# Three PSUM banks for the first layer's products, and a bank shared by two tiles of the second

## The chip, the cores and the metric

One core of a Trainium2 chip runs the kernel. The metric is the device time of one execution in microseconds; the median of several runs is given.

## The reference

```python
def _attn_ref(x, filt_r, filt_i):          # x: 8 x 2496 x 256
    X = np.fft.rfft(x, axis=1)
    Y = X * (filt_r + 1j * filt_i)[None, :, :]
    return np.fft.irfft(Y, n=x.shape[1], axis=1).astype(np.float32)

def _moe_ref(x, w_gate, w_noise, noise, w1, w2):   # x: 19968 x 256, 8 experts, 1024 hidden
    noisy_logits = x @ w_gate + np.log1p(np.exp(x @ w_noise)) * noise
    top2 = np.argpartition(-noisy_logits, 2, axis=1)[:, :2]
    ...                                    # top2_w: softmax of the two logits
    for e in range(E):
        for k in range(2):
            mask = top2[:, k] == e
            h = np.maximum(x[mask] @ w1[e], 0.0)
            out[mask] += top2_w[mask, k, None] * (h @ w2[e])
```

A filter along the sequence (FFT, product, inverse FFT) gives 19968 rows of 256. Each row then goes through two of eight experts, each a layer of 256 x 1024, a relu, and a layer of 1024 x 256.

## The kernel before

The FFT is done as matrix products, batch by batch (eight batches), and its rows are written to a DRAM table `y`. Routing makes, for each expert, lists of rows. The expert part (`expert`) then works through these lists in blocks of 512 rows (`nt` = 4 tiles of 128), all of one expert. A list entry holds one such block, in a later stage two with the same weights (a pair, the second has `i` = 1), and at the end what is left over is done in units of 256 rows (`nt` = 2). For each block:

- `gather`: POOL fetches the rows of `y` with indirect DMAs, one a tile (line 954), into eight slots of `stage`. `front` loads the weights and `turn` transposes the rows on TensorE (PE, line 970, bank `xps`); ACT and DVE take the result to SBUF.
- Layer one: for each f of 0 to 7, 128 of the 1024 hidden units, six matmuls make a product of 128 x 512. All operands are split in a high and a low part, and a product is high x high, low x high and high x low (`_mm3`, lines 119 to 121), for two halves of the 256 inputs. ACT applies the relu and writes the high part `hh` (line 1051), DVE computes the low part `hl` (line 1052), and both read the product's PSUM bank. With every second f, ACT and DVE split a quarter of the second layer's weights (`wsplit`, lines 1014 and 1015), if the block is the first with these weights.
- `turn` or `front` of the next block.
- Layer two: for each tile t of 128 rows, 24 matmuls (3 for each f) add up in one PSUM tile of 128 x 256 (`yps`). ACT reads it, scaled by the gate, into one of six slots `yo` of `stage` (line 1073), and POOL adds it to the output with an indirect DMA (line 1074). "Reading" or "scatter" below mean these two.

PSUM has eight banks of 128 x 512 floats. The names (tags) hold them so: `hps` two, `yps` two, `xps` one, `fps` three. A tile of half a bank takes a whole one. After the early part the FFT and the routing use `fps` alone. In the units, odd f take `fps` too, under the name `hq`, so that the first layer there has up to five banks.

The order in which each engine does its instructions is fixed when the kernel is built. Tile, the library below, walks a simulated timeline (`schedule_with_timeline_sim=True`): whenever an engine is free in it, the instruction that comes first in the program among those that are ready there goes next. So instructions of layer two, of the next block or of the FFT stand in PE's queue between those of layer one where the simulated bank was not free. On the chip the queues run in that order, and an instruction waits for what it needs. The same library gives out the banks of a tag and puts in the waits.

FFT steps are handed out between the expert steps (`run`, at each `yield` of `expert`), by a pace that counts these steps.

Of the kernel before, what the change touches and what calls it, by code (L numbers as in the profile page):

```python
# [10 lines left out]
F32 = mybir.dt.float32  # L11
# [9 lines left out]
NB, S, D = 8, 2496, 256  # L21
# [96 lines left out]
def _mm3(nc, o, lh, ll, rh, rl, start=True, stop=True):  # L118
    nc.tensor.matmul(o, lh, rh, start=start, stop=False)  # L119
    nc.tensor.matmul(o, lh, rl, start=False, stop=False)  # L120
    nc.tensor.matmul(o, ll, rh, start=False, stop=stop)  # L121


def f32v(ap):
    return ap.bitcast(F32)
# [13 lines left out]
class Moe:  # L139
# [885 lines left out]
    def expert(self, parts, may, fill=None):  # L1025

        nc, P = self.nc, self.P
        self.parts, self.ahead = parts, []
        self.fetch(lambda: True)
        cur = None  # L1030
        while self.ahead:
            blk, i, xg = self.ahead.pop(0)
            lt, n, nt, s, tabi, ready = blk
            w = 128 * nt
            if cur is None:
                cur = self.front(blk, xg, fill)
            w1, xT, w2st = cur
            if i == 0:
                w2, adds = [], []
            ids, gate = lt[:, i], xT[2]  # L1040
            self.fetch(may)
            hh = []
            for f in range(8):
                p = (self.ps("hq") if nt < 4 and f % 2 else self.PS.tile([128, 512], F32, name="hps", bufs=2))[:, :w]
                for kc in range(2):
                    wh, wl = w1[f // 2]
                    o = (f % 2) * 128
                    _mm3(nc, p, wh[:, kc, o:o + 128], wl[:, kc, o:o + 128], *xT[kc], start=(kc == 0), stop=(kc == 1))
                h = P.tile([128, 512], R32, name="hh", bufs=8)[:, :w]
                l = P.tile([128, 512], R32, name="hl", bufs=8)[:, :w]  # L1050
                nc.scalar.activation(h, p, AF.Relu)  # L1051
                nc.vector.scalar_tensor_tensor(l, p, 0.0, f32v(h), op0=ALU.max, op1=ALU.subtract)  # L1052
                hh.append((h, l))
                if f % 2 and i == 0:
                    w2.append(self.wsplit(w2st[f // 2], "w2", f // 2))
                yield
            late = not self.ahead
            if late:
                self.fetch(lambda: True)
            if self.ahead:  # L1060
                b2, i2, x2 = self.ahead[0]
                cur = (w1, self.turn(x2, nt), None) if i2 else self.front(b2, x2, fill if late else None)
            self.fetch(may)
            yield
            for t in range(nt):
                p = self.PS.tile([128, D], F32, name="yps", bufs=2)
                for f in range(8):
                    h, l = hh[f]
                    wh, wl = w2[f // 2]
                    _mm3(nc, p, h[:, t * 128:(t + 1) * 128], l[:, t * 128:(t + 1) * 128], wh[:, f % 2], wl[:, f % 2],  # L1070
                         start=(f == 0), stop=(f == 7))
                o = self.slot("yo")
                nc.scalar.activation(o, p, AF.Copy, scale=gate[:, t])  # L1073
                a = nc.gpsimd.indirect_dma_start(  # L1074
                    out=self.io["out"][:BLK + ready * ROWS], out_offset=bass.IndirectOffsetOnAxis(ap=ids[:, t:t + 1], axis=0),
                    in_=o, in_offset=None, compute_op=ALU.add)
                for q in adds:
                    self.tc.declare_no_dep(a.ins, q.ins, reason="distinct rows of one expert")
                adds.append(a)
                self.lasta = a  # L1080
                yield
# [108 lines left out]
```

## Time and profile before

| | |
|---|---|
| runs shown | 2447.89, 2452.72, 2455.28 us; median 2452.72 |
| the profiled execution | 2450.5 us, its span 2448.7 us |
| granted TensorE clock, mean | 0.988 |
| instructions in the profile | 43571 |
| busy: PE, DVE, ACT, POOL | 2336.5, 1471.5, 1183.8, 949.0 us |
| HBM | 219.38 MB read, 103.08 MB written |

The profile shows one execution. PE is TensorE's matmuls and PEld its weight loads, DVE is VectorE, ACT ScalarE, POOL GpSimd. A row of a group has the line, the engine, the operation, what it writes and reads (`out<-in`), the shapes, the count, and then busy time, the mean of one in ns, and the idle time of the engine ahead of it with what ended it. The names of buffers have no numbers, so the two `yps` banks look alike. A row of the waits has the waiting engine and instruction, what it waited for, and us in total, how often, and the longest. Matmuls overlap: one of 256 columns shows 0.28 us, but the next starts 0.12 us after it; one of 512 columns shows 0.39 us, and the next starts 0.23 us after it.

### The profile page before, as it was taken

How to read it: one execution, taken by the hardware profiler on the slowest of the kernel's cores; microseconds unless marked ns; L12 is line 12 of the kernel's file. 1: busy time of each engine (PE TensorE's matmuls, PEld its weight loads, DVE VectorE, ACT ScalarE, POOL GpSimd, SP SyncE). 2: the span in 40 equal slices, each digit the busy share in tenths (PEclk: the TensorE clock that was granted, in tenths of full speed). 3: DMA queues.
4: the chain of work that ended last, by engine and by line, in shares of the span. 5: the costliest groups of instructions: out<-in, count | busy, mean ns of one | idle time of the engine just before them, and what ended most of it. 6: DMA issues, size and time to landing. Idle time of an engine off the chain costs nothing. (4 is left out here: it accounts for less than half of the span.)

```text
span 2448.7 us, 43571 instructions
## 1 busy us (share of the span) xinstructions
PE 2336.5 (95%) x15299; PEld 2047.7 (84%) x15299; DVE 1471.5 (60%) x3243; ACT 1183.8 (48%) x2364; POOL 949.0 (39%) x837
## 2 busy tenths in 40 slices
PE   8878989989999999999999999999999999999998
PEld 6547877878888888887888888888888888999998
DVE  5868787787687567668668333334333434446775
ACT  5454645645554554553544344333333444446775
POOL 3123332323333333333333434453445344545553
PEclk9989999999999999999999999999999999999999
DMA  8265746746646555544544344443444344558774
GB/s 268 85 194 151 197 122 167 199 110 187 151 112 152 132 141 129 131 129 101 118 121 93 79 87 90 89 85 85 94 85 87 86 93 101 140 140 231 223 220 96
DMA packets 276350, 324.60 MB, mean 133 GB/s; under 512 B 36870, under 2 KB 189086, under 8 KB 276126
## 3 DMA queue, kind: packets, MB, share of 16 engines
q1 hardware_dynamic: 214046, 236.30, 31.9%
q0 software_dynamic: 62080, 85.47, 20.9%
q8 instruction: 122, 2.00, 0.3%
q14 instruction: 102, 0.84, 0.1%
HBM read 219.38 MB, written 103.08 MB: 132 GB/s over the span
## 5 line engine op out<-in xcount | busy, mean ns | idle before, releaser
L119 PE MATMUL yps<-w2h,hh 128*128 128x256 f32 x2560 | 717.0, 289 | 24.8 <-ACT hh L1051 24.7
L1052 DVE SCALAR_TENSOR_TENSOR hl<-hps,hh 128x512 fp32r<-128x512 f32 (+1 forms) x640 | 417.3, 656 | 534.8 <-ACT hh L1051 467.5
L120 PE MATMUL yps<-w2l,hh 128*128 128x256 f32 x2560 | 703.0, 283 | 0.0
L1074 POOL DMA_INDIRECT out<-stage,ids x320 | 527.0, 1647 | 380.9 <-ACT stage L1073 312.1
L954 POOL DMA_INDIRECT stage<-y,ids x320 | 330.6, 1033 | 872.0 <-PE xps L970 492.0
L121 PE MATMUL yps<-w2h,hl 128*128 128x256 f32 x2560 | 645.1, 283 | 1.3 <-DVE hl L1052 1.2
L1051 ACT ACTIVATE hh<-hps 128x512 fp32r<-128x512 f32 (+1 forms) x640 | 363.8, 574 | 343.4 <-PE hps L121 328.4
L119 PEld LDWEIGHTS yps<-w2h,hh 128*128 128x128 f32 x2560 | 489.7, 191 | 47.9 <-ACT hh L1051 32.4
L119 PE MATMUL hps<-mxh,w1h 128*128 128x512 f32 (+1 forms) x1280 | 489.2, 391 | 26.1 <-DVE hl L1052 21.2
L121 PEld LDWEIGHTS yps<-w2h,hl 128*128 128x128 f32 x2560 | 478.6, 191 | 36.2 <-DVE hl L1052 2.1
L120 PE MATMUL hps<-mxl,w1h 128*128 128x512 f32 (+1 forms) x1280 | 497.3, 389 | 0.1
L120 PEld LDWEIGHTS yps<-w2l,hh 128*128 128x128 f32 x2560 | 490.1, 192 | 8.0
L121 PE MATMUL hps<-mxh,w1l 128*128 128x512 f32 (+1 forms) x1280 | 492.9, 385 | 0.0
L1073 ACT ACTIVATE stage<-yps,gt 128x256 f32<-128x256 f32 x320 | 142.7, 474 | 400.8 <-issue 185.1
L119 PEld LDWEIGHTS hps<-mxh,w1h 128*128 128x128 f32 x1280 | 243.4, 191 | 70.0 <-DVE hl L1052 32.2
L121 PEld LDWEIGHTS hps<-mxh,w1l 128*128 128x128 f32 x1280 | 242.7, 190 | 43.6
L120 PEld LDWEIGHTS hps<-mxl,w1h 128*128 128x128 f32 x1280 | 242.9, 190 | 26.3 <-DVE mxl L975 0.5
L1015 DVE TENSOR_TENSOR w2l<-stage,w2h 128x512 fp32r<-128x512 f32 x216 | 141.1, 687 | 66.5 <-ACT w2h L1014 63.0
L1014 ACT CAST w1h<-stage 128x512 fp32r<-128x512 f32 x180 | 111.7, 621 | 116.2 <-PE hps L120 85.2
L1015 DVE TENSOR_TENSOR w1l<-stage,w1h 128x512 fp32r<-128x512 f32 x180 | 123.3, 686 | 66.2 <-ACT w1h L1014 65.4
L975 DVE TENSOR_TENSOR mxl<-xps,mxh 128x512 fp32r<-128x512 f32 (+1 forms) x178 | 112.8, 634 | 71.0 <-ACT mxh L974 70.1
L974 ACT CAST mxh<-xps 128x512 fp32r<-128x512 f32 (+1 forms) x178 | 96.9, 544 | 119.5 <-PE xps L970 62.7
(212 smaller groups left out, 2794.3 us busy)
## 6 DMA issues: line engine op xcount, KB each, us to landing
stage<-w SPq DMA_DIRECT2D x396, 256.0 KB
x<-x SPq DMA_DIRECT2D x88, 256.0 KB
wb<-w SPq DMA_DIRECT2D x18, 1024.0 KB
out<-z SPq DMA_DIRECT2D x24, 702.0 KB
fd<-c SPq DMA_DIRECT2D x66, 240.0 KB
fx<-fd SPq DMA_DIRECT2D x120, 128.0 KB
y<-yt SPq DMA_DIRECT2D x40, 248.6 KB
y<-yt SPq DMA_DIRECT2D x40, 234.0 KB
```

What stands on the lines that cost most here:

```text
L119: nc.tensor.matmul(o, lh, rh, start=start, stop=False)
L120: nc.tensor.matmul(o, lh, rl, start=False, stop=False)
L121: nc.tensor.matmul(o, ll, rh, start=False, stop=stop)
L954: self.pin(lambda: self.nc.gpsimd.indirect_dma_start(out=x, out_offset=None, in_=self.y[:BLK + ready * ROWS], in_offset=bass.IndirectOffse ...
L974: nc.scalar.copy(h, q[:, :w])
L975: nc.vector.tensor_sub(l, q[:, :w], f32v(h))
L1014: nc.scalar.copy(h, sv)
L1015: nc.vector.tensor_sub(l, sv, f32v(h))
L1051: nc.scalar.activation(h, p, AF.Relu)
L1052: nc.vector.scalar_tensor_tensor(l, p, 0.0, f32v(h), op0=ALU.max, op1=ALU.subtract)
L1073: nc.scalar.activation(o, p, AF.Copy, scale=gate[:, t])
L1074: a = nc.gpsimd.indirect_dma_start(out=self.io["out"][:BLK + ready * ROWS], out_offset=bass.IndirectOffsetOnAxis(ap=ids[:, t:t + 1], axis= ...
```

## The change

In layer one, f = 2 and f = 5 take a bank of the tag `yps`, in blocks and in units alike; the other six take `hps`, and `hq` is gone. In layer two, tiles 0 and 1 of a block share one PSUM tile of 128 x 2 x 256, a whole bank, and tiles 2 and 3 the next one; ACT reads each half when its 24 matmuls are done. The number of banks of each tag stays.

```diff
             for f in range(8):
-                p = (self.ps("hq") if nt < 4 and f % 2 else self.PS.tile([128, 512], F32, name="hps", bufs=2))[:, :w]
+
+                p = self.PS.tile([128, 512], F32, name="hps", tag="hps" if f % 3 < 2 else "yps", bufs=2)[:, :w]
                 for kc in range(2):
...
             for t in range(nt):
-                p = self.PS.tile([128, D], F32, name="yps", bufs=2)
+
+                if t % 2 == 0:
+                    bank = self.PS.tile([128, 2, D], F32, name="yps", bufs=2)
+                p = bank[:, t % 2]
                 for f in range(8):
```

## The prediction

> **What bounds the kernel now.** I read the busy shares first, then the stretches by stage, then who waited for whom on TensorE, and last the order of single instructions around one such wait.
>
> ```profile
> PE 2336.5 (95%) x15299; PEld 2047.7 (84%) x15299; DVE 1471.5 (60%) x3243; ACT 1183.8 (48%) x2364; POOL 949.0 (39%) x837
> 0.00:200.00 200.00, 159.66 (x913) 107.92 (x914) 141.24 (x432) 103.25 (x205) 47.59 (x50) 0.95 0.60 179
> 200.00:700.00 500.00, 470.82 (x2975) 402.95 (x2974) 374.43 (x817) 268.35 (x525) 174.28 (x148) 0.98 0.62 161
> 700.00:1400.00 700.00, 684.62 (x4429) 596.06 (x4428) 475.11 (x1174) 325.79 (x639) 251.23 (x215) 0.99 0.50 119
> 1400.00:2050.00 650.00, 633.60 (x4048) 568.93 (x4048) 243.28 (x372) 252.63 (x479) 287.03 (x255) 1.00 0.41 88
> 2050.00:2190.00 140.00, 140.00 (x909) 127.09 (x908) 69.32 (x108) 68.99 (x132) 66.42 (x58) 1.00 0.57 134
> 2190.00:2449.00 259.00, 247.85 (x2033) 244.76 (x2032) 168.11 (x343) 164.82 (x387) 122.40 (x112) 0.99 0.67 190
> ```
>
> The columns of a stretch are its length, then busy time of PE, PEld, DVE, ACT and POOL, the granted clock, the DMA share and GB/s. PE is the bound from 200 us on. The experts run beside the FFT until 1400, alone in pairs of blocks until 2050, in single blocks until 2190 and in units of 256 rows to the end. From 2050 on PE has no idle time (the last stretch ends in the write-out). So the change can only win what PE idles between 200 and 2050, and only the part that waits for a bank or for the engines that empty one. Here are PE's own waits, for the three stretches in order, two rows each, and after them the same two waits on the weight loads over the whole run (us in total, times, longest).
>
> ```profile
> PE hps L119 <- DVE hl L1052: 14.0, 12, 3.1
> PE yps L119 <- ACT hh L1051: 3.9, 7, 1.3
> ...
> PE yps L119 <- ACT hh L1051: 6.0, 6, 1.7
> PE hps L119 <- DVE hl L1052: 4.7, 6, 1.8
> ...
> PE yps L119 <- ACT hh L1051: 14.8, 14, 1.2
> PE hps L119 <- DVE hl L1052: 1.6, 5, 0.4
> ...
> PEld yps L119 <- ACT hh L1051: 32.4, 31, 2.0
> PEld hps L119 <- DVE hl L1052: 32.2, 49, 3.3
> ```
>
> A first-layer product that waits for DVE's `hl` wants its bank back. A second-layer product that waits for ACT's `hh` has been put in early, as filler between first-layer products. Together PE lost 17.9, 10.7 and 16.4 us, 45.0 in all, and 64.6 counted on the weight loads, which stop first. These two sums are the ends of what can be won.
>
> How such a filler comes to wait is seen in one pair of blocks (start, duration, and in brackets idle time before):
>
> ```profile
> 1595.60 0.28 PE L121 MATMUL yps<-w2h,hl 128*128 128x256 f32 x1
> 1595.97 0.47 ACT L1073 ACTIVATE stage<-yps,gt 128x256 f32<-128x256 f32 x1 [3.31 <-issue]
> 1598.48 0.28 PE L121 MATMUL yps<-w2h,hl 128*128 128x256 f32 x1
> 1598.69 1.59 POOL L1074 DMA_INDIRECT out<-stage,ids  x1 [0.30 <-issue]
> 1599.53 0.60 PE L970 MATMUL xps<-ident,stage 128*128 128x128 f32 x4
> 1600.25 0.47 ACT L1073 ACTIVATE stage<-yps,gt 128x256 f32<-128x256 f32 x1 [3.81 <-PE hps L121]
> 1600.62 0.59 ACT L1051 ACTIVATE hh<-hps 128x512 fp32r<-128x512 f32 x1
> 1601.27 0.38 PE L119 MATMUL yps<-w2h,hh 128*128 128x256 f32 x1 [1.14 <-ACT hh L1051]
> ```
>
> At 1595.60 the third tile of a block ends, and ACT reads it 0.09 us after the matmul's end. The fourth ends at 1598.76, but ACT reads it only at 1600.25, as POOL's scatter of 1598.69 comes to its end. The relu behind it on ACT's queue is late by that much, both `hps` banks are full, and the next thing written into PE's order is a second-layer product that needs this relu. PE stands 1.14 us.
>
> **The change part by part.** *The third bank for layer one.* No matmul, evacuation or DMA is added or taken away: f = 2 and 5 of a block move from `hps` (or from `fps`, in units) to `yps`. A full bank costs this:
>
> ```profile
> 1632.39 0.39 PE L119 MATMUL hps<-mxh,w1h 128*128 128x512 f32 x1
> 1633.09 0.39 PE L119 MATMUL hps<-mxh,w1h 128*128 128x512 f32 x1
> 1633.55 0.39 PE L121 MATMUL hps<-mxh,w1l 128*128 128x512 f32 x1
> 1633.97 0.60 ACT L1051 ACTIVATE hh<-hps 128x512 fp32r<-128x512 f32 x1 [1.50 <-PE hps L121]
> 1634.61 0.69 DVE L1052 SCALAR_TENSOR_TENSOR hl<-hps,hh 128x512 fp32r<-128x512 f32 x1 [1.41 <-ACT hh L1051]
> ```
>
> Three matmuls are issued in 0.70 us, so a product of six takes 1.40. The last one leaves PE's issue at 1633.55 + 0.23 = 1633.78, DVE is done at 1635.30: 1.52 us to empty a bank. With two banks one product (1.40) stands between a bank's use and its reuse, which is 0.12 too little, and so filler has to stand there: both first tiles of layer two in turn. With three banks two products stand there, 2.80 us, and 1.28 us of lateness costs nothing. The first layer then needs no filler, and no filler has to wait for the first relu. A lateness like the one above (1600.25 against about 1598.85, 1.40 us) would cost 0.1 instead of 1.14. Behind this stands the load of ACT and DVE in a denser first layer: 0.60 + half a weight cast on ACT, 0.69 + half a split on DVE for each 1.40 us:
>
> ```profile
> L1014 ACT CAST w2h<-stage 128x512 fp32r<-128x512 f32 x52 | 29.7, 628 | 0.0
> L1015 DVE TENSOR_TENSOR w2l<-stage,w2h 128x512 fp32r<-128x512 f32 x52 | 32.7, 685 | 1.1 <-issue 1.1
> ```
>
> That is 0.91 on ACT and 1.03 on DVE, fine where they do nothing else. Beside the FFT, DVE is 68 to 75% busy already (475.11 of 700, 374.43 of 500), and there a third bank only puts off the moment when DVE is the limit. So I take shares that fall with DVE's load. Between both counts (PE's waits, and these scaled by 64.6 / 45.0) the three stretches hold about 22, 13 and 20 us. I take a third of the first, half of the second and nine tenths of the last: 7 + 6.5 + 18 = 31.5 us.
>
> *The paired bank of layer two.* Tiles 0 and 1, and 2 and 3, now lie in one bank. No row of this trace shows an engine reading one half of a bank while PE writes the other. At the low end the second tile does not wait at all. At the high end it waits from the end of the first tile until ACT has read it: from 1595.60 + 0.12 to 1595.97 + 0.47, 0.72 us. How many such handoffs:
>
> ```profile
> L1074 POOL DMA_INDIRECT out<-stage,ids x320 | 527.0, 1647 | 380.9 <-ACT stage L1073 312.1
> L121 PE MATMUL hq<-mxh,w1l 128*128 128x256 f32 x144 | 39.0, 282 | 0.0
> ```
>
> 144 / 8 = 18 units of two tiles; (320 - 36) / 4 = 71 blocks of four; 2 x 71 + 18 = 160 handoffs, from 0 to 160 x 0.72 = 115 us. The nearest rows are those of a handoff that is there already, as tile 2 takes tile 0's bank:
>
> ```profile
> 1591.46 0.40 PE L121 MATMUL yps<-w2h,hl 128*128 128x256 f32 x2
> 1591.69 0.39 PE L119 MATMUL hps<-mxh,w1h 128*128 128x512 f32 x1
> 1591.82 0.84 ACT L1073 ACTIVATE stage<-yps,gt 128x256 f32<-128x256 f32 x2
> 1592.38 0.62 PE L119 MATMUL hps<-mxh,w1h 128*128 128x512 f32 x2
> 1592.84 0.28 PE L119 MATMUL yps<-w2h,hh 128*128 128x256 f32 x1
> ```
>
> Tiles 0 and 1 end, PE goes on with five products of the next block's first layer, and tile 2 starts at 1592.84, about 0.55 us after ACT left tile 0 (1591.82 + 0.47). The planner, which orders the queues at build time, fills this gap and leaves room. After the change tile 2 (in the other bank) and the next block's f = 0 and 1 are there as filler. I take 0.05 us a handoff, 8 us. What is queued behind a waiting matmul is everything on PE, which is why an uncovered one would cost its full length; ACT's read and POOL's scatter come after it and only shift.
>
> The Trainium skill, PSUM — Partial Sum Buffer, section "PSUM bank collisions raise a hardware error", says that PSUM must be guarded by bank and quadrant and not by address, disjoint columns included; by that rule the second tile always waits and the sum starts from the 115 us, less what filler covers. The same page, "The four PSUM rules", says that two accumulation groups open in one bank must not both clear it; by that rule tiles 0 and 1 can't run side by side as filler any more, as they do now, one matmul each in the row of 1591.46. No run here shows either so far.
>
> *Units.* They lose `hq` (the three `fps` banks) and go from five banks to three, in a stretch without any idle time.
>
> ```profile
> L1051 ACT ACTIVATE hh<-hq 128x256 fp32r<-128x256 f32 x72 | 28.1, 390 | 0.0
> L1052 DVE SCALAR_TENSOR_TENSOR hl<-hq,hh 128x256 fp32r<-128x256 f32 x72 | 29.8, 413 | 0.0
> ```
>
> Emptying takes 0.39 + 0.41 and the gaps of the block above (1.52 - 1.29), about 1.03 us; two products of half width in between are 1.40. It is covered with 0.37 to spare; I take 1 us, and 0.7 for the last unit's handoff, after which there is no filler.
>
> Sum: -31.5 + 8 + 1.7 = -21.8, against the profiled execution's 2450.5 us: 2428.7. The runs' median, 2452.72, lies 2.2 above it, less than such a run tells from another. Predicted: 2429 us.
>
> **The rivals.** *The handoff is not covered (slower).* Place: between the tiles of a pair, in every block. For it: PE's order is fixed when the kernel is built, and the lateness of 1.40 us seen at 1600.25 would hit a handoff with 0.72 of its own, and POOL's scatters fill 527.0 us of the span, a fifth of it. Against it: the 0.55 us of room at 1592.84. At 0.35 us a handoff, 56 us are lost: 2450.5 - 31.5 + 56 + 1.7 = 2477. It decides from 30 / 160 = 0.19 us a handoff.
>
> *The wait only moves (no change).* The fourth tile's read stays ahead of the next block's relu on ACT's queue, and with half the filler PE comes to the next dependence earlier. For it: ACT's lateness comes from POOL or PE's signal, not from banks. Against: the single blocks from 2050 to 2190 have the same banks and no idle time at all, so order alone can avoid it. Half of the 31.5 is kept and pays the 9.7 and some 5 more: 2450.
>
> *All of it goes.* 64.6 us less the 9.7: 2396. Against it are the long waits (3.1 us) beside the FFT, where DVE is the cause.
>
> **How the numbers follow.** Forecast 0.48, own range 2412 to 2444; uncovered handoff 0.24; wait moves 0.18; all of it 0.10. The range runs from near the last rival to the first: 2400 to 2478. 0.3% is 7.4 us, about what a measurement of this kernel can tell from no change. Faster 0.58, same 0.18, slower 0.24.
>
> **What would show it.** Right: in 1400:2050 the rows of `yps` waiting for `hh` are gone and six first-layer products follow each other without second-layer ones between; idle PE there falls from 16.4 us to a few; the stretch is about 18 us shorter. The handoff shows as `yps` L119 waiting for ACT's L1073, under 10 us in all. Wrong: that wait reaches 30 us, or idle time appears in the units, or DVE's `hl` waits beside the FFT grow because the denser first layer outruns DVE.

## The result, and the profile after

The change takes 2393.13 us (2391.52 to 2394.16, four runs); the kernel before took 2450.77 us beside it (2447.89 to 2455.28, four runs). The ratio is 0.9755, with an interval from 0.9739 to 0.977. The gain is 57.6 us; 21.8 were forecast, and the time lies 7 us below the low end of the range. It is nearly the 2396 of the third rival, that all of the waiting goes; the part on the prediction says how much of that is luck.

First the busy shares and the stretches of the kernel after, on the same borders as those of before (length, busy time of PE, PEld, DVE, ACT and POOL, granted clock, DMA share, GB/s):

```profile
span 2391.2 us, 43611 instructions
PE 2323.1 (97%) x15299; PEld 2038.2 (85%) x15299; DVE 1468.7 (61%) x3243; ACT 1177.3 (49%) x2364; POOL 934.2 (39%) x837
200.00:700.00 500.00, 485.34 (x3126) 417.98 (x3125) 372.82 (x810) 270.46 (x531) 179.97 (x157) 1.00 0.64 162
700.00:1400.00 700.00, 697.72 (x4514) 608.82 (x4513) 441.07 (x998) 326.45 (x642) 273.25 (x234) 1.00 0.51 120
1400.00:2050.00 650.00, 650.00 (x4232) 583.90 (x4231) 303.27 (x608) 271.50 (x527) 284.30 (x254) 1.00 0.45 99
```

PE's idle time in the three stretches was 29.2, 15.4 and 16.4 us, and is 14.7, 2.3 and 0.0. Over the whole span, span less PE's busy time was 112.2 us and is 68.1: 44.1 of the 57.5 us of span. The other 13.4 us lie in PE's busy time itself, 2336.5 before and 2323.1 after, with the same 15299 matmuls. They go with the granted clock, 0.98 and 0.99 in the first two rows before and 1.00 in both now: worked out from the trace's clock records, PE ran at half clock for 34.1 us between 200 us and the end of its work before, in pieces of 3.41 us or twice that, and for 3.4 us after. So 30.7 us at half clock, worth about 15 us, are gone.

PE's own waits in the kernel after, in the first two stretches; in the third no wait is listed at all:

```profile
PE hps L119 <- DVE hl L1053: 3.1, 5, 1.4
PE yps L119 <- ACT stage L1077: 1.9, 1, 1.9
PE yps L119 <- ACT hh L1052: 1.6, 1, 1.6
...
PE hps L119 <- DVE hl L1053: 1.8, 4, 0.7
```

The two waits that the forecast counted held 17.9, 10.7 and 16.4 us. They hold 4.7, 1.8 and 0 now, and 38.5 of the 45.0 us are gone, also beside the FFT. (In the kernel after, the relu stands on line 1052, `hl` on 1053, the reading on 1077 and the scatter on 1078.) The handoff within a pair would show as `yps` waiting for line 1077. By the groups it is small:

```profile
L119 PE MATMUL yps<-w2h,hh 128*128 128x256 f32 x2560 | 728.8, 288 | 4.9 <-ACT stage L1077 2.5
L119 PE MATMUL hps<-mxh,w1h 128*128 128x512 f32 (+1 forms) x1424 | 522.7, 379 | 10.0 <-DVE hl L1053 7.6
```

That is 2.5 us over the whole run, in two waits, and only the smaller is such a handoff. It takes 0.6 us and stands at 2377.4 us, before the second tile of the last unit. The larger, of 1.9 us at 242.5 us, stands before the same matmul in kernels without pairs too (2.2 us in the one with the third bank alone, below).

Next the order of single instructions, in a pair of blocks of the kernel after (start, duration, idle time before):

```profile
1572.98 1.90 POOL L1078 DMA_INDIRECT out<-stage,ids  x1 [0.30 <-ACT w2h L1014]
1573.16 0.28 PE L121 MATMUL yps<-w2h,hl 128*128 128x256 f32 x1
1573.28 0.28 PE L119 MATMUL yps<-w2h,hh 128*128 128x256 f32 x1
...
1573.88 0.28 PE L121 MATMUL yps<-w2h,hl 128*128 128x256 f32 x1
1574.00 0.39 PE L120 MATMUL hps<-mxl,w1h 128*128 128x512 f32 x1
...
1574.69 0.47 ACT L1077 ACTIVATE stage<-yps,gt 128x256 f32<-128x256 f32 x1 [0.59 <-PE hps L121]
1574.69 0.40 PE L121 MATMUL hps<-mxh,w1l 128*128 128x512 f32 x1
1574.93 0.39 PE L119 MATMUL hps<-mxh,w1h 128*128 128x512 f32 x1
```

The tile that ACT reads here began at 1571.12 and ends with its 24th matmul, that of 1573.88, at 1574.16. ACT has been idle for 0.59 us when it reads the tile at 1574.69, 0.53 us after the tile's end, while POOL's scatter of 1572.98 runs to 1574.88. In the example of before the same kind of lateness, 1.49 us (1598.76 to 1600.25), cost PE 1.14 us. It is still there, here shorter, and PE goes on without a pause.

### The profile page after: what moved, and what is told of

Read it like the earlier page. It is cut to its first block, busy times and chain, and to the rows that moved or that the text cites. A ratio compares the mean times of both kernels' runs of the same rounds, so it can differ in the third digit from the quotient of the medians.

```text
span 2391.2 us, 43611 instructions
## 1 busy us (share of the span) xinstructions
PE 2323.1 (97%) x15299; PEld 2038.2 (85%) x15299; DVE 1468.7 (61%) x3243; ACT 1177.3 (49%) x2364; POOL 934.2 (39%) x837
## 4 chain that ended last, share of the span: by engine, by line
PE 86%; DVE 6%; DMA 3%; issue 2%; ACT 2%; POOL 0%; SPq 0%; POOLq 0%; DVEq 0%; ACTq 0%
PE yps L119 12%; PE yps L121 12%; PE yps L120 12%; PE hps L119 12%; PE hps L120 11%; PE hps L121 11%; PE xps L970 3%; PE q L411 2%; PE q L475 1%; PE u L422 1%; DVE oc L883 1%; DVE hl L1053 1%; PE ra L888 1%; DMA x<-x 1%; DMA stage<-w 1%
## 5 line engine op out<-in xcount | busy, mean ns | idle before, releaser
L120 PE MATMUL yps<-w2l,hh 128*128 128x256 f32 x2560 | 719.7, 284 | 0.0
L121 PE MATMUL yps<-w2h,hl 128*128 128x256 f32 x2560 | 708.7, 284 | 0.5 <-DVE hl L1053 0.5
L1053 DVE SCALAR_TENSOR_TENSOR hl<-hps,hh 128x512 fp32r<-128x512 f32 (+1 forms) x712 | 437.9, 630 | 363.9 <-ACT hh L1052 337.4
L119 PE MATMUL hps<-mxh,w1h 128*128 128x512 f32 (+1 forms) x1424 | 522.7, 379 | 10.0 <-DVE hl L1053 7.6
L120 PE MATMUL hps<-mxl,w1h 128*128 128x512 f32 (+1 forms) x1424 | 530.2, 374 | 0.0
L121 PE MATMUL hps<-mxh,w1l 128*128 128x512 f32 (+1 forms) x1424 | 528.5, 373 | 0.0
L1052 ACT ACTIVATE hh<-hps 128x512 fp32r<-128x512 f32 (+1 forms) x712 | 381.3, 555 | 201.1 <-PE hps L121 187.4
L119 PEld LDWEIGHTS hps<-mxh,w1h 128*128 128x128 f32 x1424 | 264.7, 189 | 58.0 <-DVE hl L1053 12.8
L121 PEld LDWEIGHTS hps<-mxh,w1l 128*128 128x128 f32 x1424 | 267.9, 188 | 45.0
L120 PEld LDWEIGHTS hps<-mxl,w1h 128*128 128x128 f32 x1424 | 268.6, 189 | 35.1
```

## The experiments

Each kernel was timed beside the kernel before on the same chip. The kernel before takes 2451 us in the runs of the result, 2451 to 2469 on three chips here (A, B and C) and 2402 on a fourth (D), so ratios are what compares across chips. The groups below share a chip where they say so.

**Which part does it.** Chip A, before 2468.95. The pairing alone:

```diff
-                p = self.PS.tile([128, D], F32, name="yps", bufs=2)
+                if t % 2 == 0:
+                    bank = self.PS.tile([128, 2, D], F32, name="yps", bufs=2)
+                p = bank[:, t % 2]
```

> Layer two as after the change (two tiles in one bank), layer one as before (two hps banks, hq in the units). Theory A, the third bank makes the gain: 2450 us, between 2440 and 2475, and PE still waits 12 us or more for hh and hl between 1400 and 2050, since nothing but filler stands between the use and reuse of a bank, and there is less of it. Theory B, the gain comes from the order of layer two that the shared bank forces (tiles 0 and 2, then 1 and 3): 2400 us, between 2390 and 2415, with the waits on hh gone.

Measured: 2469.96 us, ratio 1.0012 (0.9995 to 1.003). PE's waits over the whole run, and then in 1400:2050, in this kernel:

```profile
PE yps L119 <- ACT hh L1052: 28.4, 26, 2.1
PE hps L119 <- DVE hl L1053: 21.3, 22, 2.9
...
PE yps L119 <- ACT hh L1052: 15.0, 12, 1.4
```

The waits of before are all there. Sharing a bank in pairs neither costs nor wins anything that can be told here.

The third bank alone, layer two as before:

```diff
-                p = (self.ps("hq") if nt < 4 and f % 2 else self.PS.tile([128, 512], F32, name="hps", bufs=2))[:, :w]
+                p = self.PS.tile([128, 512], F32, name="hps", tag="hps" if f % 3 < 2 else "yps", bufs=2)[:, :w]
```

> Layer one as after the change (f = 2 and 5 from yps), layer two as before, each tile in a bank of its own, so that six tiles of a block take turns on two yps banks. Theory A: 2400 us, between 2390 and 2410, with the waits on hh and hl as small as after the change. Theory B: 2440 us or more. Theory C, both parts are needed, because unpaired tiles keep both yps banks away from layer one: 2415 to 2440, with hps waiting for ACT's reading of yps.

Measured: 2393.73 us, ratio 0.9704 (0.9665 to 0.9743). The same two waits over the whole run, in this kernel, the wait at 240 us named above, and the stretch 1400:2050:

```profile
PE hps L119 <- DVE hl L1052: 6.8, 9, 2.0
PE yps L119 <- ACT hh L1051: 3.2, 3, 2.5
PE yps L119 <- ACT stage L1073: 2.2, 1, 2.2
1400.00:2050.00 650.00, 650.00 (x4228) 582.01 (x4227) 302.71 (x608) 271.00 (x528) 285.89 (x254) 1.00 0.45 99
```

The third bank alone is the whole gain. The change itself wasn't run on chip A; the next kernel differs from it in the units alone.

The change, with the first layer's banks in the units as before:

```diff
-                p = self.PS.tile([128, 512], F32, name="hps", tag="hps" if f % 3 < 2 else "yps", bufs=2)[:, :w]
+                p = (self.PS.tile([128, 512], F32, name="hps", tag="hps" if f % 3 < 2 else "yps", bufs=2) if nt == 4
+                     else self.ps("hq") if f % 2 else self.PS.tile([128, 512], F32, name="hps", bufs=2))[:, :w]
```

> The change for the blocks of 512 rows only; the units of 256 rows keep their odd products in fps (hq), but their two tiles share a bank. If the units gain or lose nothing (as A and B both say, they had no idle time before): 2393 us, between 2389 and 2398. If the fewer banks of the units cost the 1 us and more that was forecast: 2388 to 2392. If the units are a part of the gain: above 2398.

Measured: 2396.36 us, ratio 0.9721 (0.9682 to 0.976), not to be told from the one above. The gain is made in the blocks.

**Is it the scatters?** Same chip. In the kernel before, each scatter becomes a plain store of the same size on SP's queue, to fixed rows, which leaves out the addition to the right ones:

```diff
-                a = nc.gpsimd.indirect_dma_start(
-                    out=self.io["out"][:BLK + ready * ROWS], out_offset=bass.IndirectOffsetOnAxis(ap=ids[:, t:t + 1], axis=0),
-                    in_=o, in_offset=None, compute_op=ALU.add)
+                a = nc.sync.dma_start(self.io["out"][t * 128:t * 128 + 128], o)
```

> The kernel before, with POOL's scatter-add of each tile replaced by a plain store that SP's queue issues, to fixed rows: the addition to the right rows is left out. TensorE's and ACT's orders stay those of before, but for a few instructions near the start and in the last unit. Theory P, PE's signals are held up while POOL makes a scatter, and that is what made ACT and the next product late: between 1400 and 2050 the waits on hh and hl fall from 16.4 us to 3 or less, and the time to 2415 to 2435. Theory Q, ACT is late because of its own queue or its slots of yo: the waits there stay at 12 us or more and the time is 2440 to 2455.

Measured: 2391.31 us, ratio 0.9707 (0.9665 to 0.9749), with two banks and with PE's and ACT's orders those of before but for three matmuls and two instructions of ACT. It is 24 us below the low end of what was expected if scatters hold up PE's signals. The stretches 200:700 and 1400:2050 of this kernel, and the larger of the two waits in 200:700:

```profile
200.00:700.00 500.00, 481.84 (x3107) 416.06 (x3108) 391.22 (x886) 276.57 (x539) 81.69 (x97) 1.00 0.56 164
PE hps L119 <- DVE hl L1052: 9.3, 10, 1.6
...
1400.00:2050.00 650.00, 650.00 (x4190) 588.07 (x4190) 257.09 (x392) 265.12 (x502) 118.81 (x153) 1.00 0.32 93
```

Two banks are enough for a PE without idle time in the late blocks, as long as POOL makes no scatters. What two banks lack is not bandwidth but room for lateness. Beside the FFT 9.3 us of waiting for `hl` stay with two banks, so there DVE does hold PE up, as the forecast said; the third bank covers most of that too (3.1 us).

The same store in the kernel after (chip B, before 2451.46):

> The changed kernel with the plain store of the experiment before (the addition to the right rows is left out), its TensorE order nearly that of the changed kernel. If a third bank is worth no more than the patience it gives against signals held up by scatters, then there is next to nothing for it to win here: 2380 to 2393 us, within 8 us of the 2391 that the plain store gave with two banks. If the third bank and the scatters are separate costs, the two gains add: below 2365 us.

Measured: 2373.77 us, ratio 0.9675 (0.9649 to 0.9701). That lies between the two cases expected, no further gain and gains that add. On that chip the change with its scatters wasn't run. Set beside the kernel above (two banks, chip A), the third bank is worth some 17 us by the times where there are no scatters, and 0.3% or some 8 us by the ratios, whose intervals overlap; where there are scatters it is worth 58 to 75 us (2450.8 to 2393.1, 2469.0 to 2393.7). The two edits overlap for the greater part.

**What in a scatter?** Chip B. First the addition is left out, so that the scatter only writes (`compute_op=ALU.add` goes, in the kernel before):

> The kernel before, with the scatters writing in place of adding: the sum of the two experts' parts is left out. The orders of TensorE and POOL are those of before, instruction by instruction. Theory P1, what holds up TensorE's signals is POOL making the scatter's descriptors, with or without the addition: the time stays within 1% of the kernel before, and the waits on hh and hl between 1400 and 2050 stay above 12 us. Theory P2, it is the addition in DRAM, or its DMA traffic: those waits fall under 4 us and the time by 40 us or more, as with the plain store (which took 78 us off on that chip).

Measured: 2515.64 us, ratio 1.026 (1.0232 to 1.0288), 64 us slower, with the orders on PE and POOL unchanged. The scatters in POOL's groups, and PE's waits over the whole run:

```profile
L1074 POOL DMA_INDIRECT out<-stage,ids x320 | 329.4, 1029 | 556.0 <-ACT stage L1073 499.1
PE yps L119 <- ACT hh L1051: 49.3, 27, 4.2
PE hps L119 <- DVE hl L1052: 30.1, 30, 3.1
```

A scatter takes POOL 1029 ns instead of 1647, and PE's two waits hold 79.4 us (45.9 over the whole run in the profile of before). Neither theory foresaw that: it isn't the addition, nor the time that POOL is busy. Then the direction is turned, a gather from the output in place of each scatter, so that nothing is written there (chip C, before 2462.05):

```diff
-                    out=self.io["out"][:BLK + ready * ROWS], out_offset=bass.IndirectOffsetOnAxis(ap=ids[:, t:t + 1], axis=0),
-                    in_=o, in_offset=None, compute_op=ALU.add)
+                    out=o, out_offset=None, in_=self.io["out"][:BLK + ready * ROWS],
+                    in_offset=bass.IndirectOffsetOnAxis(ap=ids[:, t:t + 1], axis=0))
```

> The kernel before, with POOL's scatter of each tile replaced by a gather of the same rows and size in the other direction, from the output into the tile's slot: nothing is written to the output. The orders of TensorE and ACT are those of before, instruction by instruction. If any indirect DMA that POOL issues holds up TensorE's signals: the time stays within 1% of the kernel before, or above it as with the scatters that did not add (2516 us), and the waits on hh stay over 10 us between 1400 and 2050. If only the writing direction does: those waits fall under 3 us and the time to 2385 to 2405, as with the plain store.

Measured: 2537.6 us, ratio 1.0297 (1.0269 to 1.0325). The larger wait in 1400:2050, which holds 14.8 us in the profile of before:

```profile
PE yps L119 <- ACT hh L1051: 30.8, 12, 3.2
```

A gather at that place holds PE up as well.

**The room for descriptors.** The kernel before, with half the room that POOL's indirect DMAs have for their descriptors (`dynamic_dma_scratch_size`, 8192 before, now 4096); and three with two buffers instead of three for `th` and `tl`, which makes place: with nothing else, with 12288, and with 12288 and the change. All on chip D.

> The kernel before with dynamic_dma_scratch_size 4096 in place of 8192, the room in SBUF for the descriptors of POOL's indirect DMAs. Every engine's order is that of before, instruction by instruction. Theory R, TensorE's signals are held up while POOL waits for room there, which is used up after the four gathers of a block: with half the room the wait begins earlier and lasts longer, PE's waits on hh grow from about 25 us to 40 or more and the time by 25 us or more. Theory S, it is something else in the scatters, not the room: within 0.5% of the kernel before.

> The kernel before with two buffers in place of three for the FFT's tiles th and tl, which makes room in SBUF for the next kernel; it is the control for that one and has the same orders. Both theories: within 1% of the kernel before, waits on hh and hl between 1400 and 2050 of 12 us or more.

> The kernel just named with dynamic_dma_scratch_size 12288, all orders unchanged against it. Theory R: the hold-ups become shorter or vanish, the waits on hh and hl between 1400 and 2050 fall under 5 us and the time to 2395 to 2425, with two hps banks. Theory S: as the control, within 0.5%.

> The changed kernel with two buffers of th and tl and dynamic_dma_scratch_size 12288. Theory R: the changed kernel bears most hold-ups anyway, so the room is worth less here than with two banks: 2375 to 2392 us, toward the 2374 that the plain store gave. Theory S: 2390 to 2402, no better than the changed kernel.

Measured, in this order: 2402.02 us (ratio 1.0001, 0.9988 to 1.0015), 2385.87 (0.9938, 0.9922 to 0.9955), 2383.29 (0.9924, 0.9907 to 0.994) and 2387.79 (0.9945, 0.9928 to 0.9962). The room changes nothing here. But the question couldn't be settled on this chip, because the untouched kernel before takes 2401.57 us on it, and nothing is held up; the 12 us of waiting that were expected with two buffers aren't there either. The kernel with 4096, whose orders are those of before on every engine but for two instructions of DVE: its busy shares, its stretch 1400:2050, the two waits in 200:700 and in 700:1400 (two rows each; none is listed in 1400:2050), the scatters, and one relu.

```profile
PE 2318.4 (97%) x15299; PEld 2039.7 (85%) x15299; DVE 1473.9 (61%) x3243; ACT 1189.4 (50%) x2364; POOL 959.1 (40%) x837
1400.00:2050.00 650.00, 650.00 (x4189) 588.09 (x4188) 258.49 (x395) 266.63 (x506) 301.74 (x263) 1.00 0.44 94
PE hps L119 <- DVE hl L1052: 11.0, 10, 1.8
PE yps L119 <- ACT hh L1051: 1.9, 4, 1.3
...
PE hps L119 <- DVE hl L1052: 1.0, 2, 0.8
PE yps L119 <- ACT hh L1051: 1.0, 2, 0.7
...
L1074 POOL DMA_INDIRECT out<-stage,ids x320 | 535.4, 1673 | 360.3 <-ACT stage L1073 286.4
...
1593.51 1.56 POOL L1074 DMA_INDIRECT out<-stage,ids  x1 [0.30 <-issue]
1593.56 0.39 PE L121 MATMUL hps<-mxh,w1l 128*128 128x512 f32 x1
1593.99 0.60 ACT L1051 ACTIVATE hh<-hps 128x512 fp32r<-128x512 f32 x1 [0.90 <-PE hps L121]
```

The scatters take POOL as long as ever (1673 ns), and ACT takes up the product 0.04 us after the end of its last matmul, in the midst of one. This is the sharpest comparison of the study: same order, same scatters, another chip (the room, too, is another, but there it makes no difference to the time), and the two waits hold 12.9, 2.0 and 0 us instead of 17.9, 10.7 and 16.4. PE's busy time is 18.1 us shorter besides. With 12288 and two buffers on this chip, the change shows no gain (2387.79 against 2383.29). The two buffers alone gain 0.6% here, with other orders on the engines; that wasn't followed further.

How late PE's signals are can be worked out from the trace, as the time from the modelled end of a matmul to the record of its semaphore's update, between 1400 and 2200 us. For a matmul that ends while POOL is in none of its indirect DMAs the median is 14 ns in every kernel. Where an update left no record, the next one is taken, and the time comes out too long. For one that ends during a scatter:

| kernel | median, ns | later than 300 ns |
|---|---|---|
| before (the profile shown above) | 488 | 61% |
| pairing alone, chip A | 659 | 70% |
| no addition, chip B | 1863 | 85% |
| half the room for descriptors, chip D | 14 | 0% |
| after (its profile above) | 15 | 32% |
| third bank alone, chip A | 195 | 43% |
| the change again, chip C (below) | 269 | 47% |

In the kernels of the table with late signals 4 to 6% of PE's updates left no record, too few to make these shares. By the same measure ACT's and DVE's updates, of which a tenth left none, have medians of 9 and 12 ns under a scatter in the kernel before, so it is above all PE's signals that are late. A second count goes by what ACT and DVE do when they have been idle for PE, from 200 us on: they are on time when they start within 0.07 us of the end of a matmul that signals, and late when they start within 0.07 us of a later record instead. Under a scatter 60 of 141 such starts are late in the kernel before, 72 of 169 in the kernel after, and none of 177 on chip D; with POOL in no indirect DMA it is 13 of 535 in the kernel before.

Where signals are late, the kernels with two banks lose time, and those with three lose little though a third to nearly half of their signals under a scatter are late as well. Where no signal is late, two banks do.

**What a handoff within a bank costs, and how many products go to `yps`.** Chip B. In the change, PE's matmuls of layer two are forced into the order of the tiles, so that tile 1 follows tile 0 with no other tile of layer two between:

```diff
+                for i in bb[n:]:                     # the matmuls of one _mm3
+                    if i.engine == nc.tensor.engine:
+                        if last[0] is not None:
+                            self.tc.add_manual_dep(i, last[0].name, ...)   # order on PE, no wait
+                        last[0] = i
```

> The changed kernel, with layer two's matmuls held in the order of the tiles on TensorE (0, 1, 2, 3), so that tile 2 can't stand between 0 and 1 and only the next block's first layer can. It prices the handoff within a shared bank. If next-block products cover it: 2392 to 2402 us, with yps waiting for ACT's reading under 8 us in all. If it is not covered, 0.35 us at each of 160 handoffs: 2440 to 2460. Full exposure at 0.72 us would be 2508.

Measured: 2398.29 us, ratio 0.9773 (0.9746 to 0.9799). The handoff's wait over the whole run:

```profile
PE yps L119 <- ACT stage L1090: 3.6, 5, 0.9
```

All five stand before the second tile of a pair. Even so the handoff is a few microseconds, 0.02 each over 160. In the change the planner keeps the tiles of a pair apart: tiles 0 and 2 first, then products of the next block, then tiles 1 and 3.

Every second product in `yps`, so that four banks are used in turn:

```diff
-                p = ... tag="hps" if f % 3 < 2 else "yps", bufs=2)[:, :w]
+                p = ... tag="yps" if f % 2 else "hps", bufs=2)[:, :w]
```

> The changed kernel with odd f in yps and even f in hps, so that first-layer products take four banks in turn. If three give enough patience (1.28 us by the forecast, against hold-ups of about 0.5 to 1.4 us): 2385 to 2398 us, no different from the change. If what is left of waits beside the FFT still comes from banks: 2375 to 2385. If layer one now keeps layer two from its banks: above 2400, with hps or yps waiting for ACT's reading of yps.

Measured: 2409.73 us, ratio 0.9825 (0.9798 to 0.9853). PE's waits from 2050 to 2400 in this kernel, where the change has two of 0.7 us in all:

```profile
PE hps L119 <- DVE hl L1053: 4.5, 17, 0.6
PE hps L119 <- ACT mxh L974: 3.2, 16, 0.2
```

The blocks are as fast as with three banks (the units begin at 2157 us, with the change at 2158), but the units take 242 us instead of 222. The two waits are 7.7 us of these 20, and neither is the wait for ACT's reading that was expected. PE's busy time over the whole run is 7.9 us longer besides (2331.0 against 2323.1). That products run ahead of ACT and DVE in a row, with no filler left, would fit, but wasn't tried.

**A version that does better.** The third bank in blocks alone, the units and layer two as before; beside it the change again. Chip C, before 2462.05.

```diff
-                p = (self.ps("hq") if nt < 4 and f % 2 else self.PS.tile([128, 512], F32, name="hps", bufs=2))[:, :w]
+                p = (self.ps("hq") if nt < 4 and f % 2 else
+                     self.PS.tile([128, 512], F32, name="hps", tag="yps" if nt == 4 and f % 3 == 2 else "hps", bufs=2))[:, :w]
```

> The third bank in the blocks of 512 rows alone (f = 2 and 5 from yps); layer two with a bank for each tile and the units with hq, both as before. It joins the blocks that gained with the units that lost nothing: the units took 219 us before and 221 to 222 in every kernel with paired tiles or three banks. Expected 2 to 3 us below the changed kernel on the same chip, 2388 to 2393 us; if the units' 3 us were a matter of chance in their order, no difference, 2393 to 2396.

> The changed kernel once more, beside the kernel above: 2393 us, between 2390 and 2397, whatever the kernel before does on this chip (it took 2451 on two and 2469 on a third). If the lateness of TensorE's signals differs from chip to chip, the changed kernel should move less than the kernel before.

Measured: 2391.42 us, ratio 0.9712 (0.9698 to 0.9727), and for the change 2399.91, ratio 0.975 (0.9736 to 0.9763). On the same chip the smaller edit is 8.5 us ahead; its units take 218.8 us and the change's 221.3, which is 2.5 of it; the other 6 stay open. The change itself came out 3 us above the 2390 to 2397 expected.

## Why the prediction was wrong

**The sign and the mechanism were right, the size was not.** Two steps failed. The first is the share of the waiting that goes: a third, a half and nine tenths of the three stretches, 31.5 us. The second is the clock, which the sum left out and which made 13.4 us (below). Of the waits themselves 13.2 of 17.9, 8.9 of 10.7 and 16.4 of 16.4 us went, about three quarters, five sixths and all. The argument for small shares was DVE's load beside the FFT, "a third bank only puts off the moment when DVE is the limit". How much of the waiting was DVE's can be read where signals are punctual: 9.3 us of `hps` for `hl` in 200:700 with plain stores and 11.0 on chip D, of 14.0 in the kernel before. That much was right. But those waits went too (3.1 us stay), with DVE as busy as before (372.82 of 500, 374.43 before): 1.28 us of patience covers most of them. That they come from bursts of work on DVE fits, but wasn't tried.

**The sum, term by term.** The gain is 35.8 us larger than forecast. With the forecast's own sizes of 22, 13 and 20 us the measured shares give 47 us instead of 31.5 (0.74 x 22 + 0.83 x 13 + 20), 15.5 of it. The clock is 13.4. The handoff is 7.4, 0.6 instead of 8. The units go the other way by 1.1. This is an estimate, since the sizes themselves were one; PE's idle time fell by 44.1 us.

**Near a rival by luck.** The third rival's 2396 takes away all of the 64.6 us counted on the weight loads and has no term for the clock. Of PE's two waits 38.5 us went, and 13.4 us came from the clock.

**The row that named the cause was read as one incident.** The prediction quotes the read at 1600.25 that comes as the scatter of 1598.69 ends, and gives the lateness as an example. It doesn't ask how often that happens. The scatters fill 527.0 us, and by the records 61% of PE's signals that fall due in one between 1400 and 2200 us come more than 0.3 us late, and on the chip without lateness some 30 of the 45.0 us of waiting aren't there (12.9 + 2.0 + 0 are). A bank that forgives 1.28 us takes most of both kinds away. The forecast's own figure for that stretch, 18 of about 20 us, was then the one that came close: 16.4.

**A term was missing.** PE's idle time was the only thing that could be won in the sum; the clock wasn't priced. The granted clock of 0.98 and 0.99 stood in the stretches that were quoted, and there lay 13 us. The half-clock pieces in the records here are 3.41 us or a multiple, but for the last one, at the end of the run. The Trainium skill, TensorE: Matmul & The Clock Gate, "Part 1: The HAM clock gate (the "warmup" mystery)", gives a window of 3413 ns, and the trace agrees. Cut on the borders of these records into windows of 3.41 us, the traces show what the pieces follow. In the kernel before, from 200 us on, all eight begin after a window in which PE was idle for 1.59 us or more, and no window at full clock with 1.51 us or less is followed by one. In the kernel after the one piece follows a window with 2.06 us, and the next largest has 1.46. In the other profiles the border is less sharp (one piece after 1.00 us, none after a window with 1.88), but every window with more than 1.88 us is followed by one. Where PE's same order waits longer, the pieces are more: 14 in the kernel without the addition and 22 in the one with gathers, against 8 before and 4 on chip D with 4096. In three of the eight windows the idle time is one of the two waits counted (1.59, 1.73 and 1.79 us, with 10.2 us at half clock behind them), and these three pieces are gone after the change and on chip D. The Trainium skill, same page, "Why this matters for your kernels", advises no idle gaps over some 3 us between bursts of matmuls; the trace doesn't bear that limit out, since these three waits were shorter. So waits cost PE's clock too. How much of the 13 us belongs to the two counted stays open, since other waits stand ahead of other pieces; on chip D, without late signals, half of the time at half clock (17.1 us) is gone with the order of before.

**The costs.** The handoff was put at 8 us, between 0 and 115; it was 0.6, at the last unit, and some 4 with the tiles forced in order. The rival in which it isn't covered fell with that. (The five products that the prediction counts ahead of 1592.84 are five matmuls, less than one product.) The Trainium skill, PSUM — Partial Sum Buffer, "PSUM bank collisions raise a hardware error", has it that PSUM must be guarded by bank and quadrant and not by address, disjoint columns included. A wait for the read of a bank's other half is there, so the trace agrees, but it is 0.6 us, and 3.6 with the tiles forced in order, and not the upper bound of 115. The units were put at 1.7 us and took 3 (222 against 219).

**By its own marks.** In 1400:2050 the `yps` waits for `hh` are gone and idle PE there went from 16.4 to 0, as foreseen. "Six first-layer products follow each other" came true only in part: tiles 0 and 2 still stand between products as filler. DVE's waits beside the FFT did not grow.

**What stays open.** What in POOL's indirect DMAs of the late kind holds PE's signals. It isn't the addition, nor the direction; the room for descriptors could not be judged, since the chip on which it was varied shows no lateness. Nor is it known why chips differ so. The records of updates differ with them: in the profile of before 166 of PE's 2825 updates and 231 of ACT's 2335 left none, in that of the kernel with 4096 on chip D none and one. Each run here has a profiled span and clock, so none shows whether the profiler has a part in the lateness. The gathers of a block's rows hold up less (13 to 20% of signals over 300 ns in the kernels with two banks on chip A and in the first profile).

## What to carry to other kernels

When a wait shows a producer's signal that comes late, count how often it does before putting a share on it: signals that come half a microsecond to two late turn a ring of buffers that nearly covers its round trip (1.40 us for 1.52 here) into a ring that stalls, and one buffer more is worth far more than its bandwidth. Add it only where the round trip is too tight: the units gained nothing from it, and four banks in turn cost 20 us there. Read the granted clock as a term of the sum: waits of under 2 us went with 3.41 us at half clock. Treat a gain that rests on late signals as one that depends on the chip, 2.5 to 3% where signals were late and none that could be seen where they weren't, in the one pair of kernels run there.

## What the hardware showed that was not expected

By their records, PE's semaphore updates came 488 ns (median; one in ten over 1.18 us) after the matmul's end while POOL ran a scatter, against 14 ns with POOL in no indirect DMA, and ACT, in the example shown, stood idle until they came; ACT's and DVE's own updates were not late (9 and 12 ns). A scatter without addition, shorter by 0.6 us on POOL, made this worse (median 1863 ns). The same instructions in the same order took 2401.57 us on one chip and 2468.95 on another, and a kernel of the same order shows no late signal on the first. The clock was halved for 3.41 us or more after single waits of PE of 1.6 to 1.8 us.
